# Four transformer layers on one core: V of two head groups, late queries and the denominators' planned transfer times are moved

## The chip, the cores and the metric

The kernel runs on 1 core of one Trainium2 chip. The metric is the device time of one execution in microseconds (us), lower is better. TensorE (PE) multiplies matrices, ScalarE (ACT) computes exponentials and copies, VectorE (DVE) does elementwise work, GpSimd (POOL) and SyncE (SP) mostly issue transfers. Each engine works through its own list of instructions in the order of the program.

## The reference, cut to what matters

Two kinds of residual block alternate, A, B, A, B, on x of 2048 x 1024 with 32 heads of 32 columns each. Both start with a layer norm and project to q, k and v.

```
A: phi_q, phi_k = [softmax(q w_phi), softmax(-q w_phi)], the same of k
   o = (phi_q @ (phi_k^T v)) / (phi_q @ sum(phi_k) + 1e-6);  x += o @ wo
B: p = softmax(q k^T / sqrt(32));  o = p @ v;                x += o @ wo
```

Block B is full softmax attention, 32 heads of 2048 x 2048 scores. The kernel calls one A with the B behind it a layer; there are two layers, index 0 and 1 in the code. The change's words "layer 1" mean index 0, the first.

## The kernel before

**Tiling.** The 2048 rows are 4 chunks of 512 (c or qc), the 32 heads are 8 groups of 4 (g), so that one group is 128 columns. x stays in SBUF, transposed. V is kept per chunk and per half of the columns (fc): V(0, c) holds head groups 0 to 3, V(1, c) groups 4 to 7. In `b_v` (L971) one chunk's V is made in pieces of 128 rows (t), from the normalised x and a slab of the weight.

**Stages of a layer.** First come keys and state of A (`a_keys`), then for each chunk A's queries, its output, the layer norm for B, K of group 0 (`b_k`) and V. Then comes `attention` (L1074). Its turns are pairs (query chunk, group), 32 of them. In layer 0, where `SIDE` is 2, chunks 0 and 1 take turns 0 to 15 (two turns per group), and chunks 2 and 3 take turns 16 to 31. A turn has 64 units of 128 keys x 512 queries for one head: a score matmul (L1120, four heads side by side in 32 rows of the array), an exponential (ACT, L1136, three units in one instruction), and the product with V and with a column of ones (L1168), which gives numerators and denominators. A few units per turn are exponentiated on DVE instead (L1050 to L1069).

**The denominators.** After each half of a turn DVE copies the sums out of PSUM into a tile T (L1184). For each turn but a layer's last the denominators are then gathered into 128 partitions by four small transfers (L1214, the list `m`), inverted by DVE (L1219, `rc`), written to DRAM (L1220, `aw`), read back spread over 32 partitions per head (L1222, `bk`), and multiplied onto the numerators by DVE (L1225). All these transfers are issued by SP.

**Fillers.** While attention runs, other matmuls are fitted between its steps, all in one PSUM bank, number 7 (`FIL`): K and queries of the coming groups, V of later groups, the output projection (`b_o`), and A's keys of the next layer. Such a filler is split over four column tiles of the array (L494, mode "c", as the product with V is), where the stage ahead of attention uses the whole array (L490, `ANY` bank). DVE empties bank 7: L935 for K and V, L943 and L959 for queries. In layer 0 the queries of chunks 2 and 3 are made early by `q_away` (L952), kept in DRAM (L961), and fetched before their turn by `q_back` (L966). Where PE would be idle for longer, dummy matmuls keep it working (L494 on `onesD`, L1407 on `zero`).

**What sets the order.** Each operation is given an engine, a reckoned duration, a latency and a priority (a due time in units in which a turn is 10). `Sched.run` (L154) plays the program through with these, always starts the ready operation with the lowest priority, and emits the instructions in the order found; on the chip nothing is reordered. For a transfer (L264 to L266) the operation that needs it becomes ready at

```
ring = max(ring, t + d) + (lat - LAT[e]) * RING
lat = LAT[e] + ring - t - d
```

with 2 us for SP as LAT, half of (kb / 200) us as the rest, kb being 2 for L1214, 8 for L1220 and 600 for L1222. So the plan has the denominators' three transfers land 2.0, 2.0 and 3.5 us after their issue, where the ring is free. A small random factor on DVE and PE durations breaks ties (`TIE`), so that any change in the number of operations also stirs the order elsewhere.

**Names that the change touches.** `VQ[layer]` (L299) has three pairs (first due time, step) behind attention's start `at` for the V fillers: V(0) columns 256 to 511, which is groups 2 and 3, V(1) columns 0 to 255 (groups 4 and 5), V(1) columns 256 to 511 (groups 6 and 7). Before, layer 0 makes all 512 columns of V(0) ahead of attention (L1315) and leaves out the first pair (L1324, `[not last:]`). `QA` (L306) is first due time and step of the late queries (L1339). `gate` (L1316) lets attention start behind the means of the last layer norm.

Of the kernel before, what the change touches and what calls it, by code (L numbers as in the profile page):

```python
# [11 lines left out]
ACT = mybir.ActivationFunctionType  # L12
# [9 lines left out]
C512 = 512  # L22
# [3 lines left out]
class Buf:  # L26


    __slots__ = ("kind", "size", "cls", "banks", "left", "at", "with_")
# [4 lines left out]


class Op:
    __slots__ = ("eng", "dur", "lat", "fn", "bufs", "prio", "mode", "ndep", "out", "t", "start", "seq", "accum", "first", "ahead", "along", "drain", "rows")

    def __init__(self, eng, dur, lat, fn, bufs, prio, mode, seq):
        self.eng, self.dur, self.lat, self.fn, self.bufs = eng, dur, lat, fn, bufs  # L40
        self.prio, self.mode, self.seq = prio, mode, seq
        self.ndep, self.out, self.t, self.start, self.accum, self.first, self.ahead, self.along, self.drain = 0, [], 0.0, None, None, False, 0.0, False, False
        self.rows = ()


LAT = {"PE": 0.2, "ACT": 0.08, "DVE": 0.1, "POOL": 0.2, "SP": 2.0, "AQ": 2.0, "GQ": 2.5}
# [7 lines left out]
class Sched:  # L54
# [11 lines left out]
    def op(self, eng, dur, fn, deps=(), bufs=(), prio=0.0, lat=None, mode=None):  # L66
        o = Op(eng, dur, LAT[eng] if lat is None else lat, fn, tuple(bufs), prio, mode, len(self.ops))
        for d in deps:
            if d is not None:
                d.out.append(o)  # L70
                o.ndep += 1
        for b in o.bufs:
            b.left += 1
        if eng == "DVE" and any(b.kind == "ps" and b.banks in ([(7,)], [(6,)]) for b in o.bufs):
            o.ahead = EVAC
        self.ops.append(o)
        return o
# [76 lines left out]
    def run(self):  # L154
# [11 lines left out]
        first = {}  # L166
# [20 lines left out]
        while left:  # L187
            moved = False
            for e in engines:
                if busy[e] > t + 1e-9 or not ready[e]:  # L190
                    continue
                skipped = []
                pick = None
                full = e == "PE" and self.live.get("E", 0) >= FULL
                while ready[e] and len(skipped) < 400:
                    item = heapq.heappop(ready[e])
                    if full and not item[3].first:
                        full = False
                        held = [i for i in ready[e] if i[3].drain] if not item[3].drain else []
                        best = min(held, key=lambda i: i[:3], default=None)  # L200
                        if best is not None and self._alloc(best[3].bufs):
                            ready[e].remove(best)
                            heapq.heapify(ready[e])
                            heapq.heappush(ready[e], item)
                            pick = best[3]
                            break
                    if item[3].along and (mode[e] != item[3].mode or item[3].rows[0] in rows) and item[3].prio > now - DUE:
                        skipped.append(item)
                        continue
                    if item[3].prio <= todo[front] + WINDOW and self._alloc(item[3].bufs):  # L210
                        pick = item[3]
                        break
                    skipped.append(item)
                for s in skipped:
                    heapq.heappush(ready[e], s)
                if pick is None and e == "PE" and self.idle is not None and self.live.get("S", 0):

                    recent = [r for r in recent if r[1] > t - SPELL]
                    worked = sum(r[1] - max(r[0], t - SPELL) for r in recent)
                    if worked >= KEEP * SPELL:  # L220
                        pass
                    elif self.bank_used[7]:

                        if accum:
                            pick = Op("PE", MM, LAT["PE"], self.idle_acc, (), 0.0, "c", 0)
                            left += 1
                    elif not self.live.get("fil", 0):
                        pick = Op("PE", MM, LAT["PE"], self.idle, (Buf("ps", 0, "idle", [(7,)]),), 0.0, "c", 0)
                        pick.bufs[0].left = 1
                        self.queue["idle"] = [list(pick.bufs), 0]  # L230
                        assert self._alloc(pick.bufs)
                        left += 1
                if pick is None:
                    continue
                if pick.first:
                    now = pick.prio
                if e == "PE":
                    recent.append((t, t + pick.dur))
                    if pick.accum is not None:
                        accum = pick.accum  # L240
                d = pick.dur
                if pick.along and (mode[e] != pick.mode or pick.rows[0] in rows):
                    d += AGAIN
                if e == "PE":
                    rows = pick.rows
                if pick.mode is not None:
                    if mode[e] is not None and mode[e] != pick.mode:
                        d += SWITCH
                    mode[e] = pick.mode
                pick.start = t  # L250
                if pick.fn not in (self.idle, self.idle_acc):
                    started[pick.prio] = started.get(pick.prio, 0) + 1
                while front < len(todo) - 1 and started.get(todo[front], 0):
                    started[todo[front]] -= 1
                    front += 1
                busy[e] = t + d
                order.append(pick)
                left -= 1
                moved = True
                n += 1  # L260
                heapq.heappush(events, (t + d, n, pick, True))
                n += 1
                lat = pick.lat
                if e in ("SP", "AQ", "GQ"):  # L264
                    ring = max(ring, t + d) + (lat - LAT[e]) * RING
                    lat = LAT[e] + ring - t - d  # L266
                heapq.heappush(events, (t + d + lat, n, pick, False))
            if moved:
                continue
# [26 lines left out]
MODEST = {"slabk", "xn1", "e1", "vp1", "pkf", "lnw1", "w2o"}  # L296
NUMS = 2
LATER = ((20, 20, 0, 0), (20, 20, 0, 0))
VQ = (((1, 4.5), (2, 8), (40, 8)), ((1, 8), (70, 9), (140, 6)))  # L299
FULL = 5  # L300
OUT = (26, 22)
EARLY = (0.0, 0.0)
DUE = 0.0
BOOST = 20.0
EVAC = 20.0
QA = (40.0, 7.0)  # L306
KVG = 0.14
QUOTA = {"pk": 3, "pv": 2, "kv": 1, "ln": 2, "mm": 4, "cmp": 2, "bc": 4, "num": NUMS, "wt": 4, "fil": 2,
         "e": 6, "vp": 6, "e1": 4, "vp1": 4, "E": 6, "q2": 3, "kt": 3, "w2": 6, "w2o": 3, "oT": 27, "T": 4, "den": 2,
# [35 lines left out]
def kernel(  # L345
# [728 lines left out]
    def attention(base, kT, vT, q_of, gate, extra):  # L1074
# [69 lines left out]
        if True:  # L1144
            for qc, g in turns:
# [45 lines left out]
                if end:  # L1191
# [24 lines left out]
                    in_=T[k][1]()[64 * (1 - k) + 32 * i:64 * (1 - k) + 32 * i + 1, :].rearrange(  # L1216
                        "r (s c) -> r s c", c=16)),
                    [T[k][2]], [c_b, T[k][0]], kb=2) for k in range(2) for i in range(2)]
                rc = op("DVE", 0.27, lambda c_v=c_v: nc.vector.reciprocal(out=c_v(), in_=c_v()), m, [c_b], prio)  # L1219
                aw = dma(prio, lambda c_v=c_v, at_d=at_d: nc.sync.dma_start(  # L1220
                    out=at_d.rearrange("h (s c) -> (h s) c", c=16), in_=c_v()), [rc], [c_b], kb=8)
                bk = dma(prio, lambda r_v=r_v, at_d=at_d: nc.sync.dma_start(  # L1222
                    out=r_v(), in_=at_d.unsqueeze(1).to_broadcast([4, 32, C512])), [aw], [d_b], kb=600)
                o_b, o_v = sb("oT", C512)
                s = [op("DVE", dve_us(512), lambda a=a, k=k, o_v=o_v, r_v=r_v, T=T: nc.vector.tensor_tensor(  # L1225
                    out=o_v()[a, :], in0=T[k][1]()[a, :], in1=r_v()[a, :], op=ALU.mult),
# [28 lines left out]
    for layer in range(2):  # L1255
# [47 lines left out]
        for c in range(NC):  # L1303
            pr = second + 20 * c
            o_b, o_v = sb("oc", G, C512)
            oc = (o_b, o_v, {})
            for hf in range(2):
                a_queries(c, hf, pr + 5 * hf, wq_s, state, oc, EARLY[layer] if c == 0 else 0.0)
            a_out(c, pr + OUT[c > 0], wo_s, oc)
            xnB[c] = layernorm(c, pr + OUT[c > 0] + 1, ANY, n=4 if c == NC - 1 else 2)  # L1310
            b_k(0, c, pr + 42 + LATER[layer][c], wk0, kT, ANY, "ACT")
            if c == 0:
                q_of[(0, 0)] = b_q(0, 0, pr + 42.5, wq0, ANY)
            for t in range(TB):
                b_v(0, c, t, pr + 43 + LATER[layer][c] + 0.1 * t, bv_s[0], vT, ANY, "ACT", 0, 256 if last else C512)  # L1315
        gate = [lnq[-1]]  # L1316
        at = second + 130

        for g in range(1, G):
            pr = at + (KP[g] if last else 10 * pos[(0, g)] - 24)  # L1320
            w = slab("w2", pr - 1, B_w[:, :, D + g * P:D + (g + 1) * P], P)
            for c in range(NC):
                b_k(g, c, pr + KGAP[layer] * c, w, kT, FIL, "DVE")
        for (fc, lo), (p0, gap) in list(zip(((0, 256), (1, 0), (1, 256)), VQ[layer]))[not last:]:  # L1324
            for c in range(NC):
                for t in (0, 2):
                    b_v(fc, c, t, at + p0 + gap * (2 * c + t // 2), bv_s[fc], vT, FIL, "DVE", lo, lo + 256, 2)
# [115 lines left out]
```

## Time and profile before

| | us |
|---|---|
| three timed runs | 2362.11, 2364.65, 2368.24 (median 2364.65) |
| the profiled execution, its own time | 2371.04 |
| its span, first to last instruction | 2369.3 |
| busy in the span: PE, ACT, DVE, POOL | 2244.7, 2049.7, 1760.2, 186.2 |
| first exponential of attention in layer 0 | 359.5 |
| last exponential of attention in layer 1 | 2356.2 |

The mean granted TensorE clock was 0.992. The profile's time line has four stages: ahead of attention in layer 0 (0 to 359), attention of layer 0 (359 to about 1280), ahead of attention in layer 1 (to about 1498), and attention of layer 1 with the last projection. A busy matmul is modelled, so PE's share is an upper value. In a line of groups the columns are: line, engine, operation, tiles and shapes, count, busy us, mean ns of one, idle us of the engine just before them with what ended it.

### The profile page before, as it was taken

How to read it: one execution, taken by the hardware profiler on the slowest of the kernel's cores; microseconds unless marked ns; L12 is line 12 of the kernel's file. 1: busy time of each engine (PE TensorE's matmuls, PEld its weight loads, DVE VectorE, ACT ScalarE, POOL GpSimd, SP SyncE). 2: the span in 40 equal slices, each digit the busy share in tenths (PEclk: the TensorE clock that was granted, in tenths of full speed). 3: DMA queues.
4: the chain of work that ended last, by engine and by line, in shares of the span. 5: the costliest groups of instructions: out<-in, count | busy, mean ns of one | idle time of the engine just before them, and what ended most of it. 6: DMA issues, size and time to landing. Idle time of an engine off the chain costs nothing.

```text
span 2369.3 us, 68373 instructions
## 1 busy us (share of the span) xinstructions
PE 2244.7 (95%) x29899; PEld 863.2 (36%) x29964; DVE 1760.2 (74%) x2274; ACT 2049.7 (87%) x1921; POOL 186.2 (8%) x280
## 2 busy tenths in 40 slices
PE   7999999999999999999999999999999999989998
PEld 4443343333323333333333434433333333333333
DVE  7987752567678878767974786588888988878664
ACT  5436559999999999999997555899999999999998
POOL 0110000000010110112222200000000000100000
PEclk9999999999999999999999999999999999999999
DMA  9210101112231221223323100111111111211111
GB/s 206 63 46 1 32 24 32 39 43 51 58 93 38 58 58 56 80 72 95 122 65 94 55 3 16 24 34 27 30 33 29 32 29 26 63 29 34 42 37 35
DMA packets 124259, 118.76 MB, mean 50 GB/s; under 512 B 60728, under 2 KB 102712, under 8 KB 123576
## 3 DMA queue, kind: packets, MB, share of 16 engines
q1 hardware_dynamic: 105848, 60.38, 9.6%
q0 software_dynamic: 16032, 51.92, 7.7%
q8 instruction: 234, 3.83, 0.7%
q10 hardware_dynamic: 2080, 2.10, 0.3%
q14 instruction: 65, 0.53, 0.1%
HBM read 78.71 MB, written 14.14 MB: 39 GB/s over the span
## 4 chain that ended last, share of the span: by engine, by line
ACT 33%; PE 26%; issue 9%; DVE 7%; DMA 6%; SPq 1%; ACTq 0%; DVEq 0%; POOL 0%; another core or an unknown queue 0%; POOLq 0%
ACT arena L1136 31%; PE psum L490 7%; PE psum L494 7%; PE psum L1168 6%; PE psum L1120 5%; DMA arena<-rd 3%; DVE arena L1225 1%; DVE arena L1066 1%; DMA rd<-arena 1%; DMA arena<-arena 1%; DVE arena L1069 1%; ACT arena L703 1%; DVE arena L1050 1%; DVE arena L1058 0%; DVE arena L1184 0%
## 5 line engine op out<-in xcount | busy, mean ns | idle before, releaser
L1136 ACT ACTIVATE arena<-psum 128x1536 bf16<-128x1536 f32 (+1 forms) x1366 | 1724.8, 1487 | 29.9 <-PE psum L1120 15.8
L1168 PE MATMUL psum<-arena 128*32 128x512 bf16 x4096 | 628.2, 386 | 8.8 <-DVE arena L1184 6.5
L1168 PE MATMUL psum<-arena,ones_bf 128*32 128x512 bf16 x4096 | 628.3, 386 | 0.0
L494 PE MATMUL psum<-arena 128*32 128x512 bf16 (+1 forms) x9792 | 597.2, 355 | 13.2 <-DVE arena L935 4.8
L1120 PE MATMUL psum<-arena 32*128 32x512 bf16 x4096 | 541.0, 383 | 69.3 <-ACT arena L1136 60.6
L490 PE MATMUL psum<-arena 128*128 128x512 bf16 (+1 forms) x1975 | 449.0, 375 | 12.4 <-issue 4.5
L1120 PEld LDWEIGHTS <-arena 32*128 32x128 bf16 x4096 | 176.0, 91 | 596.8 <-issue 588.5
L1066 DVE SCALAR_TENSOR_TENSOR arena<-arena 128x1024 f32<-128x1024 f32 x282 | 343.8, 1219 | 3.8 <-PE psum L1168 0.6
L494 PEld LDWEIGHTS <-arena 128*32 128x32 bf16 x9792 | 221.9, 96 | 240.3 <-issue 128.7
L490 PEld LDWEIGHTS <-arena 128*128 128x128 bf16 x2032 | 190.3, 98 | 247.4 <-issue 45.6
L1050 DVE TENSOR_SCALAR arena<-psum 128x512 int32<-128x512 f32 x282 | 192.6, 687 | 110.0 <-PE psum L1120 98.9
L1168 PEld LDWEIGHTS <-arena 128*32 128x32 bf16 x4096 | 161.0, 95 | 231.3 <-issue 187.2
L1069 DVE SCALAR_TENSOR_TENSOR arena<-arena 128x1024 bf16<-128x1024 f32 x141 | 172.0, 1220 | 7.9 <-DVE arena L1066 0.4
L1168 PEld LDWEIGHTS <-ones_bf 128*32 128x32 bf16 x4096 | 158.0, 95 | 32.0 <-issue 16.7
L935 DVE CAST arena<-psum 128x512 bf16<-128x512 f32 x120 | 82.3, 686 | 97.1 <-PE psum L494 94.5
L596 POOL DMA_DIRECT2D arena<-in_B_wqkv_dram x46 | 41.5, 903 | 1322.2 <-PE psum L494 338.8
L1225 DVE TENSOR_TENSOR arena<-arena 64x512 bf16<-64x512 f32 x124 | 84.8, 684 | 61.6 <-DMA arena<-rd 55.5
L494 PE MATMUL psum<-xT,onesD 128*32 128x512 bf16 x1236 | 116.5, 385 | 1.5 <-DVE arena L1005 1.3
L703 ACT ACTIVATE arena<-psum 128x512 bf16<-128x512 f32 x80 | 43.1, 599 | 82.2 <-PE psum L490 60.6
L1184 DVE COPY arena<-psum 128x512 f32<-128x512 f32 x126 | 86.5, 686 | 29.3 <-PE psum L1168 28.4
L1061 DVE TENSOR_SCALAR arena<-arena 128x1024 int32<-128x1024 int32 x141 | 98.9, 702 | 4.4
L1058 DVE TENSOR_SCALAR arena<-arena 128x1024 int32<-128x1024 int32 x141 | 97.6, 692 | 3.3 <-PE psum L1168 0.3
(109 smaller groups left out, 1486.7 us busy)
## 6 DMA issues: line engine op xcount, KB each, us to landing
arena<-rd SPq DMA_DIRECT2D x62, 256.0 KB
arena<-in_B_wqkv_dram POOLq DMA_DIRECT2D x58, 256.0 KB, 4.1
arena<-in_B_wo_dram POOLq DMA_DIRECT2D x40, 256.0 KB, 3.9
arena<-arena SPq DMA_DIRECT2D x256, 32.0 KB
arena<-wd_k POOLq DMA_DIRECT2D x32, 256.0 KB, 4.8
arena<-in_A_wqkv_dram POOLq DMA_DIRECT2D x32, 256.0 KB, 4.2
arena<-arena SPq DMA_DIRECT2D x96, 64.0 KB
out_dram<-arena SPq DMA_DIRECT2D x32, 128.0 KB
```

What stands on the lines that cost most here:

```text
L490: nc.tensor.matmul(out_, lhsT=lhsT, rhs=rhs, start=start, stop=stop, skip_group_check=True)
L494: nc.tensor.matmul(out_[ks, :], lhsT=lhsT[:, ks], rhs=rhs, start=start, stop=stop, tile_position=(0, 32 * k), skip_group_check=True)
L1050: o = op("DVE", dve_us(512), lambda: nc.vector.tensor_scalar(out=y_v()[:, k, :].bitcast(I32), in0=s_v()[:, x * C512:(x + 1) * C512], scala ...
L1058: mo = op("DVE", 1024 / 1920 + 0.15, lambda: nc.vector.tensor_scalar(out=m_v().bitcast(I32), in0=y_v().bitcast(I32), scalar1=0x7FFFFF, sca ...
L1061: po = op("DVE", 1024 / 1920 + 0.15, lambda: nc.vector.tensor_scalar(out=y_v().bitcast(I32), in0=y_v().bitcast(I32), scalar1=0x7F800000, s ...
L1066: last = [op("DVE", dve_us(1024), lambda i=i, c=c: nc.vector.scalar_tensor_tensor(out=x_v(), in0=(x_v() if i else m_v()), scalar=c, in1=m_ ...
L1069: return op("DVE", dve_us(1024), lambda: nc.vector.scalar_tensor_tensor(out=e_v(), in0=x_v(), scalar=POW2_0, in1=y_v(), op0=ALU.add, op1=A ...
L1120: nc.tensor.matmul(out=s_v()[:, x * C512:(x + 1) * C512], lhsT=kT[g][1]()[r, pp, d * P:(d + 1) * P], rhs=q_of[(qc, g)][1]()[r, (pp + j // ...
L1136: ex = op("ACT", act_us(w * C512), lambda s_v=s_v, e_v=e_v, w=w: nc.scalar.activation(out=e_v(), in_=s_v()[:, 0:w * C512], func=ACT.Exp, s ...
L1168: nc.tensor.matmul(out=a_v()[col:col + 32, :], lhsT=v_v()[:, kc % 4, o:o + DH] if what == 0 else ones_bf[:], rhs=ev()[:, x * C512:(x + 1) ...
L1184: cp = op("DVE", dve_us(512), lambda t_v=t_v, a_v=a_v: nc.vector.tensor_copy(out=t_v(), in_=a_v()), [last], [a_b, t_b], prio - 4)
L1225: s = [op("DVE", dve_us(512), lambda a=a, k=k, o_v=o_v, r_v=r_v, T=T: nc.vector.tensor_tensor(out=o_v()[a, :], in0=T[k][1]()[a, :], in1=r_ ...
```

## The change

Three things. In layer 0, V of groups 2 and 3 is no longer made ahead of attention but as fillers, eight pieces of 256 rows x 256 columns, as layer 1 has it already; the fillers for groups 4 to 7 are given later due times. The late queries get due times from 90 in steps of 6 instead of from 40 in steps of 7. And operations get a field `slack`, which the plan adds to a transfer's landing: 1.5 us for L1214, 1.0 for L1220, 2.5 for L1222, in both layers. The transfers themselves are the same.

```diff
-    __slots__ = (..., "drain", "rows")
+    __slots__ = (..., "drain", "rows", "slack")
...
+        self.slack = 0.0
...
                     ring = max(ring, t + d) + (lat - LAT[e]) * RING
-                    lat = LAT[e] + ring - t - d
+                    lat = LAT[e] + ring - t - d + pick.slack
...
-VQ = (((1, 4.5), (2, 8), (40, 8)), ((1, 8), (70, 9), (140, 6)))
+VQ = (((1, 4.5), (36, 4), (70, 6)), ((1, 8), (70, 9), (140, 6)))
...
-QA = (40.0, 7.0)
+QA = (90.0, 6.0)
...
                     [T[k][2]], [c_b, T[k][0]], kb=2) for k in range(2) for i in range(2)]
+                for o in m:
+                    o.slack = 1.5
...
+                aw.slack, bk.slack = 1.0, 2.5
...
-                b_v(0, c, t, pr + 43 + LATER[layer][c] + 0.1 * t, bv_s[0], vT, ANY, "ACT", 0, 256 if last else C512)
+                b_v(0, c, t, pr + 43 + LATER[layer][c] + 0.1 * t, bv_s[0], vT, ANY, "ACT", 0, 256)
...
-        for (fc, lo), (p0, gap) in list(zip(((0, 256), (1, 0), (1, 256)), VQ[layer]))[not last:]:
+        for (fc, lo), (p0, gap) in list(zip(((0, 256), (1, 0), (1, 256)), VQ[layer])):
```

The line numbers of the profile of before are used throughout; behind the second added line the changed file's are 1 higher, and behind the lines added in `attention` 4 higher.

More of the change, by code (lines that the diff above doesn't have):

```diff
@@ L36 @@
 class Op:
-    __slots__ = ("eng", "dur", "lat", "fn", "bufs", "prio", "mode", "ndep", "out", "t", "start", "seq", "accum", "first", "ahead", "along", "drain", "rows")
+    __slots__ = ("eng", "dur", "lat", "fn", "bufs", "prio", "mode", "ndep", "out", "t", "start", "seq", "accum", "first", "ahead", "along", "drain", "rows", "slack")
     def __init__(self, eng, dur, lat, fn, bufs, prio, mode, seq):
```

## The prediction

> **What bounds the kernel now.** I read the busy time by stretch first, then who waited for whom, then the time line where waits follow each other.
>
> ```profile
> 240.00:350.00 110.00, 108.72 (x646) 44.41 (x658) 76.85 (x104) 57.92 (x92) 8.13 (x10) 1.00 0.10 27
> 350.00:460.00 110.00, 108.45 (x1673) 44.19 (x1672) 35.21 (x51) 103.91 (x83) 0.95 (x2) 1.00 0.13 34
> 460.00:560.00 100.00, 97.36 (x1561) 37.89 (x1564) 68.43 (x88) 99.62 (x80) 6.65 (x7) 1.00 0.19 49
> 660.00:760.00 100.00, 91.29 (x1244) 30.25 (x1242) 79.98 (x102) 96.02 (x80) 11.24 (x15) 1.00 0.24 69
> ```
>
> The columns of a stretch are its length, then busy us of PE, weight loads, DVE, ACT, POOL, the clock, and the transfers. Ahead of attention (first row) ACT is half idle and PE full: PE bounds. In attention, from 359.5 on, ACT is at 96 to 100% and bounds; PE is close behind in the first turns (108.45 of 110, 97.36 of 100), less so later (91.29). So a gain can come from less PE work ahead of attention, or from what ACT still idles in attention. These are ACT's waits, first in attention of layer 0 (460 to 1275 us), then of layer 1 (1495 to 2345); us in total, times, longest:
>
> ```profile
> ACT arena L1136 <- PE psum L1120: 7.2, 10, 1.6
> ACT arena L1136 <- PE psum L1168: 4.3, 5, 2.3
> ACT arena L1136 <- DVE arena L1225: 2.2, 2, 1.4
> ACT arena L1136 <- DMA qd<-arena: 1.8, 1, 1.8
> ACT arena L1136 <- issue: 1.1, 3, 0.6
> ...
> ACT arena L1136 <- PE psum L1120: 8.6, 12, 1.6
> ACT arena L1136 <- issue: 2.3, 1, 2.3
> ACT arena L1136 <- DVE arena L1225: 1.1, 1, 1.1
> ```
>
> That is 16.6 us and 12.0 us, 28.6 in all. What starts it is seen on DVE, in the groups of the denominators:
>
> ```profile
> L1225 DVE TENSOR_TENSOR arena<-arena 64x512 bf16<-64x512 f32 x124 | 84.8, 684 | 61.6 <-DMA arena<-rd 55.5 <-DMA arena<-arena 2.5 <-PE psum L1168 1.7
> L1219 DVE RECIPROCAL arena<-arena 128x16 f32<-128x16 f32 x62 | 15.3, 247 | 28.2 <-DMA arena<-arena 25.9 <-DMA qd<-arena 2.3
> ```
>
> DVE stood 86.2 us (55.5 + 2.5 + 25.9 + 2.3) at the head of its list for these transfers. DVE itself has room, but what is queued behind empties bank 7 and computes DVE's exponentials. One such case on the time line, DVE, then PE, then ACT:
>
> ```profile
> 597.53 1.40 DVE L1225 TENSOR_TENSOR arena<-arena 64x512 bf16<-64x512 f32 x2 [2.52 <-DMA arena<-arena]
> 598.96 0.69 DVE L935 CAST arena<-psum 128x512 bf16<-128x512 f32 x1
> 599.71 0.61 PE L494 MATMUL psum<-arena 128*32 128x512 bf16 x8 [2.35 <-DVE arena L935]
> 600.85 1.45 ACT L1136 ACTIVATE arena<-psum 128x1536 bf16<-128x1536 f32 x1 [1.57 <-PE psum L1120]
> ```
>
> The copy out of bank 7 is late, the next filler stands for it, and the scores behind the filler starve ACT. Going through both attentions, I counted the ACT idle that lies within 10 us behind a DVE wait of 0.9 us or more for a transfer: 31 pieces, the first and the last of them with their DVE waits being
>
> ```profile
> 488.11 1.39 DVE L1225 TENSOR_TENSOR arena<-arena 64x512 bf16<-64x512 f32 x2 [1.76 <-DMA arena<-rd]
> 489.57 2.79 ACT L1136 ACTIVATE arena<-psum 128x1536 bf16<-128x1536 f32 x2 [0.38 <-PE psum L1168]
> ...
> 2077.21 0.68 DVE L1225 TENSOR_TENSOR arena<-arena 64x512 bf16<-64x512 f32 x1 [4.07 <-DMA arena<-rd]
> 2082.12 2.37 ACT L1136 ACTIVATE arena<-psum 128x1536 bf16<-128x1536 f32 x2 [0.40 <-PE psum L1120]
> ```
>
> They hold 15.2 us in layer 0 and 9.8 in layer 1, 25.0 of the 28.6, though 40 stretches of 10 us are but a quarter of the 1665 us.
>
> **Part 1: V ahead of attention.** The order of the built programs says what moves: 128 of the full-array matmuls of 512 columns ahead of attention become 128 of 256 columns, and 512 column-tiled ones of 256 columns join the fillers. The end of the stage on the time line:
>
> ```profile
> 338.10 1.89 PE L490 MATMUL psum<-arena,onesD 128*128 128x512 bf16 x8
> 339.83 19.16 PE L490 MATMUL psum<-arena 128*128 128x512 bf16 x87
> 342.09 0.63 ACT L576 ACTIVATE arena<-arena 128x512 f32<-128x512 f32 x1
> 348.68 1.22 DVE L586 TENSOR_TENSOR arena<-arena 128x1024 bf16<-128x1024 f32 x1
> 359.51 13.55 ACT L1136 ACTIVATE arena<-psum 128x1536 bf16<-128x1536 f32 x10
> ```
>
> A full-array matmul takes 19.16 / 87 = 0.220 us, so one of half width 0.110. Before, 88 of them stand between the last layer norm's matmuls and the first scores; after, 24 of half width. That is 88 x 0.220 - 24 x 0.110 = 16.7 us. Ahead of that layer norm another 12 in full-width terms go, 2.6 us. So the first scores come 19.3 us sooner. What was passed follows in the first turn (8 full, 32 half: 5.3 us), K of chunk 3 among it, as scores of the ninth step need it: the normalised chunk is done at 349.9 - 2.6 = 347.3, and two matmuls, a copy and a transfer (3.3 us as below) make that about 353; ACT, which first has to finish the layer norm (342.7 - 2.6) and two half copies, starts its exponentials near 341, and eight of them at 13.55 / 10 = 1.36 us reach 352, so this wait is at most 1 us.
>
> Counted from the built order, PE's fillers of turns 0 to 12 grow by the work of 25 filler groups (four column tiles of 512 each), these stragglers included: 25 x 0.22 = 5.6 us. If PE bounds these turns, the stage brings 19.3 - 5.6 = 13.7 us; if ACT does, 19.3 less five copies on ACT (one of 0.59, four of half that width, 0.38) and the wait, 16 us. I take **13.7**, as PE has hardly a gap there. Behind turn 12 the rest hides: 104 of the dummy matmuls fall away, and the eight more copies on DVE (0.69 each) fit where DVE is at 80%.
>
> ```profile
> L934 ACT CAST arena<-psum 128x512 bf16<-128x512 f32 x24 | 14.1, 587 | 20.7 <-PE psum L490 19.6 <-PE psum L811 1.1
> L934 ACT CAST arena<-psum 128x256 bf16<-128x256 f32 x16 | 5.9, 382 | 12.7 <-PE psum L490 12.7
> L494 PE MATMUL psum<-arena 128*32 128x256 bf16 x2560 | 93.5, 275 | 0.6 <-DVE arena L935 0.6
> 594.20 3.31 DMA arena<-arena
> ```
>
> As fillers V costs PE more than it did ahead: 93.5 x 4 / 2560 = 0.146 us for four column tiles, so 128 x 0.146 = 18.7 us against 14.1. This is the upper bound of what the move can cost, if nothing hides it.
>
> A rule speaks against mixing: the Trainium skill, TensorEngine Tiling (Array Packing), Tiling Modes, says that a change of tiling mode drains the array. The trace agrees: three scores start at 361.07 and the filler behind them at 361.39, 0.32 us for 0.22 of work.
>
> ```profile
> 361.07 0.39 PE L1120 MATMUL psum<-arena 32*128 32x512 bf16 x3
> 361.39 0.61 PE L494 MATMUL psum<-arena 128*32 128x512 bf16 x8
> ```
>
> But fillers ride in the mode of the product with V, and the built order has only 8 more changes of mode in attention of layer 0 and 14 more in layer 1: 2 us by 0.1 each, which I leave to the range.
>
> **Part 2: late queries.** Same 16 pieces; by DVE's order their copies move from turns 3 to 13 to turns 8 to 18, and K, V and queries of the first turns get the place. V of groups 6 and 7 is done by turn 11 and needed in turn 12. Nothing is added, so 0, with the rival below.
>
> **Part 3: the reckoned transfers.** One denominator's chain, from the chain of waits:
>
> ```profile
> 671.55 4.35 DMA arena<-arena
> ...
> 676.65 0.26 DVE arena L1219
> 676.94 2.66 DMA rd<-arena
> 679.73 4.92 DMA arena<-rd
> 684.78 0.68 DVE arena L1225
> ```
>
> The plan reckons 2.0, 2.0 and 3.5 us for the three transfers; they take 4.35, 2.66 and 4.92. With the slack it reckons 3.5, 3.0 and 6.0, in sum 12.5 against 11.9 measured. In the orders of the two programs I added up DVE's work (durations by group) that is placed between copy and reciprocal, and between reciprocal and product:
>
> | mean DVE work, us | before, layer 0 / 1 | after, layer 0 / 1 |
> |---|---|---|
> | last copy to reciprocal | 2.4 / 2.3 | 3.9 / 4.1 |
> | reciprocal to product | 5.9 / 6.4 | 7.9 / 9.3 |
>
> The chain needs 5.1 (671.55 to 676.65) and 7.9 us (676.9 to 684.78). Taking the mean gain in work off each of DVE's waits leaves some 11 of the 86 us. For ACT's 25.0 us I take three quarters in layer 1, **7.4**, and half in layer 0, **7.6**, since there PE lacks the room to catch up in the first turns. Bounds: nothing, and all 25.0.
>
> **Sum.** 13.7 + 7.6 + 7.4 = 28.7 us. The profiled execution took 2371.04 (span 2369.3, 1.7 us around it), so 2342.3. The runs' median is 2364.65, 0.3% below that execution; taken off it, **2336 us**.
>
> **Rivals.**
>
> - *Only the stage's gain remains* (0.10). DVE's waits on transfers go, but ACT's idle stays because PE is what starves it: 13.7 less 2 us for changes of mode gives 2353. For: ACT's waits name L1120, a matmul, most often. Against: 25.0 of 28.6 us lie behind a DVE wait. A rule would make it so in another way: the Trainium skill, DMA: Bandwidth & Descriptors, Anatomy of one DMA, fits 2.0 us plus bytes / 436 GB/s for transfers issued by GpSimd, by estimate 2.6 us for the 256 KB read back. Then 2.66 + 2.6 us would lie within the 5.9 us of work, and there would be no wait to take away. The measured 4.92 us and DVE's 55.5 us of waits decide against it.
> - *PE gives V back* (0.08). If PE bounds to the end of layer 0's attention, V costs 18.7 us there against 14.1 ahead, and layer 0's idle stays; with layer 1's 7.4 that is 2364.65 + 4.6 - 7.4 = 2362. For: PE at 95%. Against: 664 dummy matmuls on L1407 alone, put where PE had nothing to do.
> - *The queue of SP, slower* (0.05). The late queries' writes now stand among their own fetches, which begin behind turn 13: by SP's order 7 of the 16 are issued there. A write takes 4.9 us and a fetch 2.3:
>
> ```profile
> 713.62 4.87 DMA qd<-arena
> 744.10 2.31 DMA arena<-qd
> ```
>
>   SP works in order, so a write that waits for its copy holds the fetch, and scores stand for it. At 7.2 us each for 7 turns that is 50 us: 2336 + 50 = 2386. It decides once a fetch is issued less than 7 us ahead of its turn; the fetches start two to three turns of 28 us ahead, so I doubt it.
> - *The plan undoes it* (0.02): V done no later than before, slack without effect, 2365. The built orders speak against it.
>
> **How the numbers follow.** Forecast 0.75 (2323 to 2350). Its low end has ACT bound the first turns and all 25.0 us gone: 2364.65 - 16 - 25 = 2324. The range reaches over the first rival and into the second: 2323 to 2360, which leaves out some 0.15. A difference of 0.3% (7 us) is what a measurement can tell. Faster: forecast 0.75 and most of the first rival, 0.83; same: the rest of it, the second and the last, 0.12; slower 0.05.
>
> **What would show it.** Right: first exponential near 341 us; waits of L1225 and L1219 for transfers near 15 us of 86; ACT's waits in attention near 14 us of 28.6; the stage ahead of attention in layer 1 as long as before. Wrong: first exponential early but ACT idle in turns 0 to 12 (PE gives V back); DVE's waits gone while ACT's stay (first rival); ACT or PE standing for qd fetches behind turn 16 (SP).

## The result, and the profile after

The changed kernel took 2334.07 us (median of 4), the kernel before 2365.03 beside it: ratio 0.9869, 95% interval 0.9852 to 0.9886, 31 us less. 2336 was forecast. Its profiled execution took 2335.27 us, its span is 2333.5.

First the start of attention in layer 0 on the changed kernel's time line (its L1121 and L1137 are the scores and the exponential, L1120 and L1136 before):

```profile
340.35 0.60 PE L1121 MATMUL psum<-arena 32*128 32x512 bf16 x6
340.88 5.49 ACT L1137 ACTIVATE arena<-psum 128x1536 bf16<-128x1536 f32 x4
```

The first exponential is at 340.9 us in place of 359.5. Then the groups of the denominators' product and reciprocal on DVE:

```profile
L1229 DVE TENSOR_TENSOR arena<-arena 64x512 bf16<-64x512 f32 x124 | 84.6, 682 | 9.9 <-DMA arena<-rd 8.0
L1222 DVE RECIPROCAL arena<-arena 128x16 f32<-128x16 f32 x62 | 15.1, 243 | 6.1 <-DMA arena<-arena 6.1
```

DVE's waits for these transfers fell from 86 to 14 us. And ACT's waits for its exponentials, first in the whole attention of layer 0 (341 to 1252 us), then of layer 1 (1468 to 2322); us in total, times, longest:

```profile
ACT arena L1137 <- PE psum L1121: 6.3, 8, 2.0
ACT arena L1137 <- PE psum L1169: 2.0, 2, 1.2
ACT arena L1137 <- issue: 1.1, 1, 1.1
ACT arena L1137 <- DMA arena<-arena: 0.6, 1, 0.6
...
ACT arena L1137 <- PE psum L1121: 2.8, 3, 1.3
...
ACT arena L1137 <- PE psum L1169: 2.2, 1, 2.2
```

That is 10.0 and 5.0 us, 15.0 in place of 28.6. Of this 4.4 us lie in the first 100 us of layer 0's attention (341 to 440), where the kernel before has no such wait:

```profile
ACT arena L1137 <- PE psum L1121: 3.2, 2, 2.0
ACT arena L1137 <- PE psum L1169: 1.2, 1, 1.2
```

For the rest of this text attention is read from two rows per kernel, busy time by stretch, each from the first exponential to the last. Columns: the stretch, its length, then busy us of PE, weight loads, DVE, ACT, POOL, the granted clock, transfers. Length less ACT's busy time is what ACT idles. Before:

```profile
360.00:1276.00 916.00, 867.49 (x13209) 314.19 (x13199) 636.76 (x808) 898.86 (x737) 118.54 (x161) 0.99 0.23 67
1492.00:2357.00 865.00, 819.67 (x12163) 302.55 (x12166) 688.02 (x870) 850.57 (x690) 23.40 (x28) 0.99 0.12 33
```

After:

```profile
341.00:1252.00 911.00, 873.70 (x13593) 328.67 (x13593) 646.19 (x822) 900.38 (x742) 119.97 (x164) 1.00 0.24 67
1252.00:1468.00 216.00, 210.03 (x1554) 89.73 (x1577) 157.38 (x216) 119.02 (x204) 16.41 (x29) 0.99 0.09 29
1468.00:2322.00 854.00, 819.81 (x12193) 305.75 (x12195) 686.79 (x869) 848.04 (x688) 24.20 (x28) 1.00 0.13 34
```

ACT's work hardly moves (898.9 to 900.4, 850.6 to 848.0); its idle goes from 17.1 to 10.6 and from 14.4 to 6.0. The stage between the two (middle row) stays at 216 us. Between the two profiled spans, 35.8 us go: 18.6 ahead of attention, 6.1 in layer 0's attention, 10.3 in layer 1's, under 1 elsewhere. (The profiled execution of before was one of its longer ones, so the spans differ by more than the medians.)

By this the prediction held, and nearly so by stages. What is not seen from one pair of kernels is whether its parts are worth what it said, since attention of layer 0 holds V's extra work, the queries' move and the slack at once.

### The profile page after: what moved, and what is told of

Read it like the earlier page. It is cut to its first block, busy times and chain, and to the rows that moved or that the text cites. A ratio compares the mean times of both kernels' runs of the same rounds, so it can differ in the third digit from the quotient of the medians.

```text
span 2333.5 us, 69138 instructions
## 1 busy us (share of the span) xinstructions
PE 2231.2 (96%) x30307; PEld 877.5 (38%) x30372; DVE 1762.5 (76%) x2282; ACT 2042.5 (88%) x1921; POOL 186.8 (8%) x280
## 4 chain that ended last, share of the span: by engine, by line
ACT 43%; PE 36%; issue 10%; DVE 8%; DMA 2%; SPq 1%; ACTq 0%; DVEq 0%
ACT arena L1137 40%; PE psum L491 18%; PE psum L495 6%; PE psum L1121 5%; PE psum L1169 5%; DVE arena L1067 2%; DMA arena<-arena 1%; ACT arena L704 1%; DVE arena L1051 1%; DVE arena L1229 1%; DVE arena L1059 1%; DVE arena L1070 1%; DVE arena L1062 1%; PE psum L737 1%; PE psum L812 1%
## 5 line engine op out<-in xcount | busy, mean ns | idle before, releaser
L1137 ACT ACTIVATE arena<-psum 128x1536 bf16<-128x1536 f32 (+1 forms) x1366 | 1722.4, 1515 | 15.3 <-PE psum L1121 9.1
L495 PE MATMUL psum<-arena 128*32 128x512 bf16 (+1 forms) x10304 | 608.6, 349 | 3.8 <-DVE arena L936 1.6
L1121 PE MATMUL psum<-arena 32*128 32x512 bf16 x4096 | 537.0, 382 | 58.3 <-ACT arena L1137 51.6
L491 PE MATMUL psum<-arena 128*128 128x512 bf16 (+1 forms) x1974 | 436.9, 368 | 15.4 <-DVE arena L587 5.2
L1121 PEld LDWEIGHTS <-arena 32*128 32x128 bf16 x4096 | 181.2, 91 | 583.7 <-issue 573.0
L495 PEld LDWEIGHTS <-arena 128*32 128x32 bf16 x10304 | 234.0, 96 | 228.5 <-issue 113.9
L1169 PEld LDWEIGHTS <-arena 128*32 128x32 bf16 x4096 | 163.2, 95 | 229.7 <-issue 184.0
L936 DVE CAST arena<-psum 128x512 bf16<-128x512 f32 x128 | 87.9, 687 | 118.8 <-PE psum L495 103.9
L704 ACT ACTIVATE arena<-psum 128x512 bf16<-128x512 f32 x80 | 43.1, 598 | 81.8 <-PE psum L491 60.1
L495 PE MATMUL psum<-xT,onesD 128*32 128x512 bf16 x1192 | 110.9, 381 | 0.4 <-DVE arena L573 0.3
L830 ACT ACTIVATE arena<-psum 128x512 bf16<-128x512 f32 x128 | 69.7, 597 | 32.9 <-PE psum L491 30.6
```

The costliest lines, as they stand in the source:

```text
L491: nc.tensor.matmul(out_, lhsT=lhsT, rhs=rhs, start=start, stop=stop, skip_group_check=True)
L495: nc.tensor.matmul(out_[ks, :], lhsT=lhsT[:, ks], rhs=rhs, start=start, stop=stop, tile_position=(0, 32 * k), skip_group_check=True)
L936: return op("DVE", dve_us(512), lambda: nc.vector.tensor_copy(out=dst(), in_=src()), [dep], bufs, prio)
L1121: nc.tensor.matmul(out=s_v()[:, x * C512:(x + 1) * C512], lhsT=kT[g][1]()[r, pp, d * P:(d + 1) * P], rhs=q_of[(qc, g)][1]()[r, (pp + j // ...
L1137: ex = op("ACT", act_us(w * C512), lambda s_v=s_v, e_v=e_v, w=w: nc.scalar.activation(out=e_v(), in_=s_v()[:, 0:w * C512], func=ACT.Exp, s ...
L1169: nc.tensor.matmul(out=a_v()[col:col + 32, :], lhsT=v_v()[:, kc % 4, o:o + DH] if what == 0 else ones_bf[:], rhs=ev()[:, x * C512:(x + 1) ...
```

## The experiments

The theory was that the slack and V's move each give, about 15 and 14 us, and add up, the queries' due times giving nothing. The rivals: one part gives all; PE gives V back; the order that the plan happened to find gives it. Times are told as the ratio to the kernel before, timed beside each; differences between kernels below are differences of ratios, times 2365 us.

| kernel | ratio | interval | median us |
|---|---|---|---|
| whole change | 0.9869 | 0.9852 to 0.9886 | 2334.1 |
| slack_only | 0.9889 | 0.9871 to 0.9907 | 2342.1 |
| v_only | 0.9997 | 0.9986 to 1.0009 | 2367.5 |
| no_slack | 1.0060 | 1.0040 to 1.0080 | 2381.6 |
| old_queries | 0.9918 | 0.9901 to 0.9935 | 2348.4 |
| slack_queries | 0.9881 | 0.9865 to 0.9897 | 2341.0 |
| seed8_before | 0.9996 | 0.9982 to 1.0011 | 2367.6 |
| seed8_slack_only | 0.9900 | 0.9885 to 0.9915 | 2345.4 |
| seed8_no_slack | 0.9975 | 0.9962 to 0.9988 | 2364.6 |
| seed8_after | 0.9829 | 0.9813 to 0.9846 | 2329.3 |
| slack_half | 0.9873 | 0.9846 to 0.9899 | 2334.9 |
| slack_double | 0.9882 | 0.9867 to 0.9897 | 2339.9 |
| queries_mid | 0.9944 | 0.9927 to 0.9961 | 2353.4 |

**slack_only**: the changed kernel with V and late queries as before.

```diff
-VQ = (((1, 4.5), (36, 4), (70, 6)), ...
-QA = (90.0, 6.0)
+VQ = (((1, 4.5), (2, 8), (40, 8)), ...
+QA = (40.0, 7.0)
...
+                b_v(0, c, t, ..., 0, 256 if last else C512)
...
+        for ... in list(zip(...))[not last:]:
```

> Before's V and late queries, with the three slack values. Theory of the prediction (both parts give, and add up): the first exponential stays at 359 us, DVE's waits on denominators' transfers fall from 86 to about 15 us, ACT's waits in attention from 28.6 to about 13, and the time falls by 15 us (9 to 22), to about 2350. Rival that moving V gives all: within 5 us of before, 2360 or more. Rival that the plan's slack gives all: about 2334, as the whole change.

It is 26 us faster than before, by itself (ratio 0.9889). Its two attentions:

```profile
359.00:1261.00 902.00, 864.72 (x13210) 314.70 (x13209) 636.59 (x808) 897.98 (x737) 119.23 (x161) 1.00 0.24 68
...
1478.00:2328.00 850.00, 814.95 (x12193) 304.18 (x12195) 686.57 (x869) 847.29 (x688) 24.28 (x28) 1.00 0.13 34
```

ACT idles 4.0 and 2.7 us, 24.8 less than before in sum. That is nearly all of what the prediction had counted behind DVE's waits (25.0), and well over the 15 it took. The rival that V gives all falls. The rival that the slack gives all is not settled by this pair: the whole change is 5 us faster, but the two intervals overlap. Only the pair with seed 8, below, differs by more than its intervals.

**v_only** and **no_slack**: the changed kernel with the three slack values at zero, and, for v_only, the queries' old due times.

```diff
-                    o.slack = 1.5
+                    o.slack = 0.0
...
-                aw.slack, bk.slack = 1.0, 2.5
+                aw.slack, bk.slack = 0.0, 0.0
```

> V of groups 2 and 3 as fillers with the new due times of the V fillers; late queries at their old due times, slack zero. Theory of the prediction: first exponential near 341 us, DVE's waits stay near 86 us, ACT's waits near 29 us or a little more, time 14 us (10 to 17) below before, about 2351. Rival that PE gives V back in attention: first exponential early too, but the time within 5 us of before.

> The whole change but for the slack, which is zero. Theory of the prediction: as V alone, about 2351, as the late queries' due times were put at nothing; the step from here to the whole change is the slack's, about 15 us. Rival that the queries' due times matter: this differs by over 5 us from V alone.

Both fail the theory. The first exponential is early in both (341 and 339 us), but attention of layer 0 gives it back, v_only first, no_slack second:

```profile
341.00:1278.00 937.00, 883.52 (x13731) 333.67 (x13727) 647.52 (x822) 902.61 (x743) 120.48 (x167) 1.00 0.23 67
```

```profile
339.00:1288.00 949.00, 889.72 (x13765) 331.88 (x13762) 648.39 (x822) 903.82 (x742) 121.08 (x163) 0.99 0.23 65
```

ACT idles 34.4 and 45.2 us where it idled 17.1. How that comes is seen in no_slack's longest piece, a chain on four engines:

```profile
707.20 0.68 DVE L1229 TENSOR_TENSOR arena<-arena 64x512 bf16<-64x512 f32 x1 [3.38 <-DMA arena<-rd]
707.81 0.68 DVE L944 TENSOR_SCALAR arena<-psum 128x512 bf16<-128x512 f32 x1
708.18 0.88 POOL L597 DMA_DIRECT2D arena<-in_B_wqkv_dram  x1 [17.66 <-DVE arena L1229]
...
713.07 1.91 PE L495 MATMUL psum<-arena 128*32 128x512 bf16 x32 [1.76 <-DMA arena<-in_B_wqkv_dram]
714.91 0.39 PE L1121 MATMUL psum<-arena 32*128 32x512 bf16 x3
...
715.44 2.79 ACT L1137 ACTIVATE arena<-psum 128x1536 bf16<-128x1536 f32 x2 [14.70 <-PE psum L1121]
```

The product waits for the denominators read back; the copy of a query out of bank 7 is behind it on DVE; POOL's load of a weight waits for the product, and PE has a filler on that weight at the head of its list. ACT gets no scores for 14.7 us. That filler is a late query's, and no V is among the fillers of this stretch. Why such delays cost more with V and queries moved than they did before is not shown by it.

no_slack is also 15 us slower than v_only, so with this seed the rival that the queries' due times matter holds: without the slack the new ones cost. Attention of layer 0 is 12 us longer (949 against 937), with that one stall in it.

**old_queries**: the whole change, slack included, with `QA = (40.0, 7.0)`.

> The whole change but for the late queries, which keep their old due times (40 in steps of 7). Theory of the prediction: within 4 us of the whole change, about 2336. Rival that PE is the bound in turns 3 to 13, where the queries then stand beside V: 6 to 14 us more than the whole change, with ACT's waits in those turns.

12 us slower than the whole change (0.9918 against 0.9869), in the upper part of the rival's range. Its attention of layer 0, and the longest piece of ACT's idle:

```profile
340.00:1267.00 927.00, 884.52 (x13771) 332.77 (x13766) 645.85 (x822) 901.41 (x744) 117.16 (x160) 1.00 0.23 66
```

```profile
526.72 0.69 DVE L936 CAST arena<-psum 128x512 bf16<-128x512 f32 x1
...
530.35 0.69 DVE L960 TENSOR_SCALAR arena<-psum 128x512 bf16<-128x512 f32 x1 [1.82 <-PE psum L495]
...
531.79 0.39 PE L1121 MATMUL psum<-arena 32*128 32x512 bf16 x3
...
534.19 0.68 DVE L1229 TENSOR_TENSOR arena<-arena 64x512 bf16<-64x512 f32 x1 [2.02 <-DMA qd<-arena]
534.80 0.68 DVE L944 TENSOR_SCALAR arena<-psum 128x512 bf16<-128x512 f32 x1
535.17 0.88 POOL L597 DMA_DIRECT2D arena<-in_B_wqkv_dram  x1 [0.30 <-DMA arena<-arena]
535.50 0.50 SPq L949 DMA_DIRECT2D arena<-arena  x1
...
539.00 0.39 PE L1121 MATMUL psum<-arena 32*128 32x512 bf16 x2
539.43 2.13 ACT L1137 ACTIVATE arena<-psum 128x1024 bf16<-128x1024 f32 x2 [5.18 <-DMA arena<-arena]
```

Over the whole kernel DVE's waits for the denominators' transfers are small here (9.5 us). V (L936) and a late query (L960) pass through bank 7 ahead of the query of the coming turn (L944). That query leaves the bank only at 534.8, behind their work and a product that stood 2.02 us. Its halves are swapped by transfers issued from 535.5 on, and no score starts between 531.8 and 539.0. ACT idles 25.6 us in this attention, 15.0 more than in the whole change; the piece shown is 5.18 of it, and what causes the others is open.

**slack_queries**: slack and the queries' new due times, V as before (edits as in slack_only, without that of QA).

> Slack and the late queries' new due times, V as before. Theory (slack keeps the plan true; the queries' move only makes room for V's fillers): ACT has just 4 us of idle in layer 0's attention with slack alone, so nothing can be won, 2342 within 4 us. Rival (the queries' due times are worth some 14 us by themselves, as old_queries against the whole change reads): 2328 or less.

Within 2 us of slack_only: the theory holds. The queries' move is worth nothing by itself. That it makes the room that V needs is read from the piece of old_queries alone.

**Seed 8**: `TIE = 8` in place of 7, which redraws the random factor of up to 1% on the plan's DVE and PE durations and so the order, in four of the kernels. It tells what an order is worth by chance.

> Slack alone with tie seed 8 in place of 7, which stirs the order but changes no work. Theory that slack keeps the plan true: 2342 within 6 us, ACT idle in both attentions below 10 us. Rival that seed 7 was a lucky order: 10 us or more slower.

> V's and the queries' move without slack, seed 8. Theory that late transfers hit a PE without room: ACT idle in layer 0's attention over 30 us again and 2365 to 2390. Rival that the one stall of 14.7 us at 715 us with seed 7 was an accident of that order: at or below the kernel before, 2350 to 2365.

> The whole change with seed 8. Theory: within 6 us of the whole change, 2328 to 2340, first exponential near 341 us. Rival that the order of seed 7 was lucky: 2345 or more.

> The kernel before with tie seed 8. Theory (slack alone is worth 20 to 30 us whatever the order): within 6 us of before, DVE's waits for the denominators' transfers 70 to 100 us, and 20 us or more above the seed 8 run with slack alone (2345). Rival that seed 7 was unlucky for before: 2355 or less.

Before (under 1 us) and slack_only (3 us) hardly move, so the slack by itself is worth 23 us with seed 8, 26 with seed 7. Without slack, V and queries cost 14 us with seed 7 and gain 5 with seed 8 (against seed8_before; the two intervals overlap): the stall of 14.7 us was in part an accident of seed 7, as the rival said, though the idle pieces before ACT's exponentials in attention of layer 0 still add up to 26.5 us. On top of the slack V and queries bring 5 us with seed 7, where the two intervals overlap, and 17 with seed 8, where they don't. The whole change with seed 8, 2329.3 us, is the fastest of all, faster than both kernels compared here. Attention of layer 0 in seed8_slack_only, then in seed8_after:

```profile
358.40:1262.60 904.20, 866.87 (x13268) 315.55 (x13267) 636.76 (x808) 897.90 (x738) 120.62 (x165) 1.00 0.24 69
...
340.80:1246.90 906.10, 870.15 (x13590) 327.30 (x13591) 646.32 (x822) 899.94 (x743) 121.38 (x163) 1.00 0.24 68
```

**slack_half**, **slack_double**: the three values halved (0.75, 0.5, 1.25) and doubled (3.0, 2.0, 5.0).

> The whole change with half the slack: the plan then reckons 10.0 us for the three transfers where 11.9 were measured. Theory that truth of the plan is what counts: waits in part left, DVE's 25 to 60 us, ACT idle 20 to 35 us in both attentions, time 2340 to 2358. Rival that any slack does: within 4 us of the whole change.

> The whole change with double the slack: the plan reckons 17.5 us for the three. Theory: DVE's waits below 8 us, little left to win, within 5 us of the whole change (2329 to 2339). Rival that holding the tiles longer costs as much as waits do: 2342 or more, with PE or DVE waiting for the copies out of the accumulator's bank.

Half the slack does as well as all (2334.9), against the theory: DVE still waits 8.3 us at the product and 13.5 at the reciprocal, but the idle pieces before ACT's exponentials add up to 12.1 and 2.5 us in the two attentions, in sum as with all of it (10.0 and 5.0). Double takes DVE's waits to 2.0 us and wins nothing: 2339.9, its interval overlapping the whole change's. So the plan need not be true, at least with V and queries moved and seed 7; by this reading what counts is that the wait no longer reaches ACT.

**queries_mid**: `QA = (65.0, 6.5)`.

> The whole change with late queries due from 65 in steps of 6.5, halfway. Theory that they compete with V for bank 7 and PE in turns 3 to 11: ACT idle in layer 0's attention 12 to 22 us, between 10 and 25 of the two ends, time 2337 to 2346. Rival that only the one order matters: outside of both ends.

Not between the ends, as the rival said: as slow as the old due times or slower (the intervals overlap). One stall makes most of it, for a new reason; POOL, PE, DVE, ACT:

```profile
660.20 1.76 POOL L597 DMA_DIRECT2D arena<-in_B_wqkv_dram  x2 [42.75 <-ACT arena L1137]
...
661.95 2.87 POOL L600 DMA_DIRECT2D arena<-wd_k  x4
...
670.55 1.40 DVE L1229 TENSOR_TENSOR arena<-arena 64x512 bf16<-64x512 f32 x2 [3.62 <-DMA arena<-in_A_wqkv_dram]
670.68 3.54 PE L495 MATMUL psum<-arena 128*32 128x512 bf16 x32 [4.87 <-DMA arena<-in_B_wqkv_dram]
...
674.27 0.69 DVE L936 CAST arena<-psum 128x512 bf16<-128x512 f32 x1 [2.32 <-PE psum L495]
...
676.00 1.94 ACT L1137 ACTIVATE arena<-psum 128x1024 bf16<-128x1024 f32 x2 [10.65 <-PE psum L1121]
```

```profile
666.00:671.00 5.00, 0.32 (x4) 0.14 (x8) 1.39 (x3) 0.00 (x0) 0.98 (x2) 0.96 1.02 296
```

A filler stood 4.87 us for its weights, which POOL had issued from 660.2 on, with loads for the next layer (wd_k and others) close behind them. The single row is busy time by stretch: from 666 to 671 the transfer engines are busy throughout (a share of 1.02, 296 GB/s), and PE and ACT stand. 10.65 us of ACT went. The product of the denominators stood 3.62 us in the same jam, but what held PE was the filler's weights.

## Why the prediction was right, and where it was not

- **V ahead of attention.** 19.3 us sooner was reckoned for the first scores and 341 us forecast for the first exponential; it came at 340.9. The net 13.7 us lies between what V and queries brought on top of the slack with the two seeds, 5 and 17. Neither seed hits it, and the step to it, PE's 5.6 us of added fillers (25 x 0.22 is 5.5), is not what the runs show. With seed 7, against slack_only, the start comes 18 us sooner, attention of layer 0 is 9 us longer, 6.6 of it ACT's idle and 2.4 ACT's own work (copies that now fall there), and attention of layer 1 is 4 us longer. 4.4 us of that idle lie in the first 100 us, where slack_only has none and the prediction allowed a wait of at most 1 us. With seed 8, against seed8_slack_only, the start comes 17.6 us sooner (358.4 to 340.8) and attention of layer 0 is only 1.9 longer (904.2 to 906.1), 15.7 in all: the 16 that the prediction gave for the case that ACT bounds.
- **The slack.** The cause was right: DVE's waits fell from 86 to 14 us (15 forecast), and ACT's idle behind them with them. The term was mis-sized: 15.0 us were taken of the 25.0 counted, 26 and 23 measured with the two seeds. The step that failed is "half in layer 0 ... since there PE lacks the room to catch up in the first turns". With slack alone ACT idles 4.0 us in layer 0, from 17.1: PE had the room, as long as its work stays what it was. The "three quarters in layer 1", 7.4 us, were too little as well: there the idle fell by 11.7, from 14.4 to 2.7. That in the whole change layer 0's idle fell by 6.5 us, near the 7.6 taken, is no proof of that step, since V and queries put idle of their own there.
- **Late queries.** "Nothing is added, so 0" failed. It holds with V as before (2341.0 against 2342.1). Beside V the due times count, though nothing is added to the work, and not in one direction: with slack the old ones cost 12 us, without slack they save 15 (v_only against no_slack), and with slack the ones halfway are no better than the old. In the pieces shown the cause is a different one each time: a place in bank 7's queue, a chain behind a late denominator, weights in a jam of transfers. All this is with seed 7 alone.
- **The sum.** 28.7 forecast, 31 measured. The parts were not independent as the sum took them. The step from no_slack to the whole change is 45 us with seed 7, from seed8_no_slack to seed8_after 35, while before to slack_only is 26 and 23. So the total came out nearer than its terms, and that was luck: with seed 7 the slack was taken 11 us too small and V 9 us too large (15.0 for 26, 13.7 for 5 on top of the slack), and the two errors nearly cancel.
- **The rivals.** *Only the stage's gain remains* fell: ACT's waits went with DVE's. With it falls the reading by which the 256 KB come back in 2.6 us. *PE gives V back* is what happens with seed 7 as soon as the slack or the queries' move is missing (v_only 0.9997, no_slack 1.0060, old_queries 0.9918 against 0.9889 for the slack alone, the intervals just overlapping), in the pieces shown by stalls at the head of the lists and not by PE's sum of work; with seed 8 and without slack 5 us were left. *The queue of SP* did not decide: in the changed kernel no wait of ACT's exponentials is put down to qd.
- **Open.** How much of the 5 or 17 us is V's and how much the order's is not settled by two seeds. Nor is it whether another pair of due times would do better than 90 and 6, or whether the old ones would cost 12 us with another seed; queries_mid shows that such differences can come from one stall.

## What to carry to other kernels

Where a list of instructions is ordered by a plan, look for the waits at the head of an engine that is not the bound: 86 us of DVE's waits cost ACT 25 us through the copies queued behind them, and reckoning those transfers a few us longer won them back without any less work. Fill a stage closer to the limit only once such waits are gone; the same move of V and queries was worth between -14 and 5 us without the slack and 5 to 17 us with it. And redraw the order at least once before the size of a small gain is believed.

## What the runs showed of the hardware that was not expected

A short stall of PE can cost more than its length. In v_only PE stood 1.81 us for a copy on DVE (until 536.22), and then the granted clock fell. Busy time by stretch of v_only (the clock is the third figure from the end), and two like fillers of 16 matmuls on either side, with the stalled matmul between them:

```profile
530.00:536.00 6.00, 4.41 (x67) 1.51 (x58) 2.01 (x4) 5.93 (x5) 0.00 (x0) 1.00 0.20 68
536.00:539.00 3.00, 2.78 (x28) 1.31 (x31) 0.94 (x3) 0.00 (x0) 1.48 (x2) 0.56 0.02 1
```

```profile
530.93 1.05 PE L495 MATMUL psum<-arena 128*32 128x512 bf16 x16
...
536.22 0.47 PE L1169 MATMUL psum<-arena 128*32 128x512 bf16 x1 [1.81 <-DVE arena L1185]
...
536.90 1.96 PE L495 MATMUL psum<-arena 128*32 128x512 bf16 x16
```

At a clock of 0.56 the same work took 1.96 us in place of 1.05. In queries_mid the filler behind the 4.87 us of waiting took 3.54 us for 32 matmuls, against 1.91 in no_slack. Not every such stall does this: in no_slack PE stood 2.11 us until 708.53, a little longer than in v_only, and the clock stayed full:

```profile
706.00:709.00 3.00, 0.89 (x20) 0.36 (x16) 1.80 (x3) 0.00 (x0) 0.82 (x1) 1.00 0.10 33
709.00:713.00 4.00, 2.31 (x44) 1.05 (x36) 3.86 (x5) 0.00 (x0) 0.06 (x1) 1.00 0.44 102
```

What decides between the two cases is not shown. Over whole spans the mean granted clock was 0.992 before, 0.991 in no_slack, 0.996 after, 0.998 in slack_only and 1.000 in seed8_after. So the kernels with fewer waits had the higher mean clock; what the clock cost in time wasn't measured by itself.
